# Attention and max-out expert kernel: heads loaded as pairs, split in place and put together by copies and on-chip transfers, with a fixed list of expert products

## Chip, cores and metric

The kernel runs on one core of one Trainium2 chip. The metric is the device time of one execution in microseconds (us); lower is better. Five engines work beside each other: PE multiplies matrices, DVE, ACT and POOL work on vectors (POOL can't read PSUM), and SP here issues nearly all transfers, in program order.

## What is computed

```python
def _attn_ref(q, k, v, s):                     # B, H, S, D = 8, 8, 576, 64
    scores = scale * np.matmul(q, k.transpose(0, 1, 3, 2))
    cum = np.cumsum(np.maximum(s, 0.0), axis=-1)
    bias = -(cum[:, :, :, None] - cum[:, :, None, :])
    scores = np.where(causal, -1e9, scores + np.minimum(bias, 0.0))
    attn = np.exp(scores - np.max(scores, axis=-1, keepdims=True))
    attn = attn / (np.sum(attn, axis=-1, keepdims=True) + 1e-09)
    return np.matmul(attn, v)
...
x = attn_out.transpose(0, 2, 1, 3).reshape(B * S, H * D)        # 4608 x 512
h = np.maximum(np.maximum(x @ w1, x @ w2), x @ w3)              # 4608 x 768
return h @ w_out                                                # 4608 x 512
```

## The kernel before

Attention goes by **visits**: a visit is one batch and one pair of heads (two heads of 64 rows fill 128 partitions). A visit has **steps**, one for each block of 128 queries (qb 0 to 4, the last of 64). Batches 0 and 1 are visited twice, once for qb 0 and 1 and once for qb 2 to 4: 16 visits, 40 steps. Batches 2 to 7 have one visit for each pair with all five blocks: 24 visits (16 to 39), steps 40 to 159. These 24 are called stacked (`stacked`), and the change is about them.

To keep precision with 16-bit products, numbers are split into a high half in fp16 and the low rest. In a stacked visit each head's scores are two products over 128 rows: tile `h` holds the head's (q low, k high) on its own 64 partitions and (q high, k high) on the other 64; tile `l` holds the bias rows on the head's own partitions and (q high, k low) on the others. So each head needs its q and k on both halves of the partitions. Before, the input `qk` has each head twice, one copy under the other. `load_head` (L139) loads 128 x 1152 floats for each head into one of two buffers `raw`; `head_qhi` (L177) and `head_khi` (L181) write the high halves on ACT; `head_qlo` (L186) writes q low on DVE, and POOL copies q high (L190); `head_klo` scales k on POOL (L195) and subtracts (L198); `head_bias` copies the bias rows on POOL. Apart from that, `load_pair` (L289) loads the same pair once more from `pair`, and `pair_max` (L298, DVE) finds its largest magnitudes, from which `pair_scale1` to `pair_scale3` make the batch's scales.

A step t runs: `probs` (reciprocal on DVE, high half of the probabilities on ACT, L716, low half on DVE, L719, then their transposes by SP, L722, and L728 for qb 4), `highest(t+1)` on DVE (L657, L652), the pending evictions, some expert products, `scores(t+2)` on PE (L555, and L566 for qb 4) with `expo(t+1)` on ACT (L676), then the preparations that are due, more expert products, and `values` (L847). Scores have two PSUM buffers, so `scores(t+2)` waits until L719 of step t has read its own.

The experts work on a batch's rows in two sets, of 256 and of 320 columns: 18 groups `pm` (L979, 12 products each), whose maxima DVE takes (L996) and POOL splits (L985, L986), and 4 groups `po` (L1021, 18 products each). How many groups run in a step is in the list `GROUPS` for steps 0 to 59, as (ahead of the scores, behind them). From step 60 on one group goes ahead of the scores and the rest while a running budget (`STEP_NS` for a step, less `pe_cost`) is positive. What is left after step 159 runs at the end.

The order of everything else is the recording order: `at(step, function, ...)` puts a preparation into a step, and the table `moved` shifts single ones by some steps. Each transfer stands in SP's queue where it was recorded, and SP waits at its head.

Of the kernel before, what the change touches and what calls it, by code (L numbers as in the profile page):

```python
# [21 lines left out]
def kernel(  # L22
# [5 lines left out]
    qk: bass.AP,  # L28
# [5 lines left out]
    nc = tc.nc  # L34
# [24 lines left out]
    STEP_NS = 4520.0  # L59
# [80 lines left out]
    def load_head(v, j):  # L140
        b, g, _ = visits[v]
        r = R.setdefault(v, {})
        if v == 2 * NP * NB:
            for n, (x, c0, c1) in enumerate((("rq", 0, S), ("rk", S, 2 * S))):
                r[x, j] = wpool.tile([P, 2 * N], F32, tag=f"w{14 + 2 * j + n}", name=f"{x}{v}_{j}")[:, 0:c1 - c0]
                nc.sync.dma_start(out=r[x, j], in_=qk[b, g, j, :, c0:c1])
            return
        t = io.tile([P, V0], F32, tag="raw", name=f"raw{v}_{j}", bufs=2)
        nc.sync.dma_start(out=t[:, 0:2 * S], in_=qk[b, g, j])
        r["rq", j], r["rk", j] = t[:, 0:S], t[:, S:2 * S]  # L150

    def head_bias(v, j):

        r = R.setdefault(v, {})
        if j == 0:
            h = att.tile([P, 2 * S], F16, tag="qkh", name=f"h{v}_0")
            if v < 2 * NP * NB + 2:
                LOW[v % 2, 0] = att.tile([P, 2 * S], F16, tag="qkl", name=f"l{v}_0")
        else:
            if v < 2 * NP * NB + 2:  # L160
                LOW[v % 2, 1] = wpool.tile([P, 2, 2 * S], F16, tag=f"w{18 + v % 2}", name=f"x{v}_1")
            h = LOW[v % 2, 1][:, 0]
        l = LOW[v % 2, 1][:, 1] if j else LOW[v % 2, 0]
        r["h", j], r["l", j] = h, l
# [8 lines left out]
        nc.gpsimd.tensor_copy(out=l[own, Q4:S], in_=qr[own, g, 4:5].to_broadcast([D, D]))

    def head_qhi(v, j):
        raw, h = R[v]["rq", j], R[v]["h", j]
        nc.scalar.activation(out=h[:, 0:S], in_=raw, func=AF.Copy, scale=QK[visits[v][0]]["q"])  # L177

    def head_khi(v, j):
        raw, h = R[v]["rk", j], R[v]["h", j]  # L180
        nc.scalar.activation(out=h[:, S:2 * S], in_=raw, func=AF.Copy, scale=QK[visits[v][0]]["k"])  # L181

    def head_qlo(v, j):
        raw, h, l = (R[v][x, j] for x in ("rq", "h", "l"))
        far, own = slice((1 - j) * D, (2 - j) * D), slice(j * D, (j + 1) * D)
        nc.vector.scalar_tensor_tensor(  # L186
            out=h[own, 0:S], in0=raw[own], scalar=QK[visits[v][0]]["q"][own], in1=h[own, 0:S],
            op0=ALU.mult, op1=ALU.subtract,
        )
        nc.gpsimd.tensor_copy(out=l[far, 0:S], in_=h[far, 0:S])  # L190

    def head_klo(v, j):
        raw, h, l = (R[v][x, j] for x in ("rk", "h", "l"))
        far = slice((1 - j) * D, (2 - j) * D)
        nc.gpsimd.tensor_scalar(  # L195
            out=raw[far], in0=raw[far], scalar1=QK[visits[v][0]]["k"][far], scalar2=None, op0=ALU.mult
        )
        nc.gpsimd.tensor_tensor(out=l[far, S:2 * S], in0=raw[far], in1=h[far, S:2 * S], op=ALU.subtract)  # L198
# [1235 lines left out]
```

## Time and profile before

| what | value |
|---|---|
| median of 3 runs | 884.27 us (882.59 to 884.44) |
| the profiled execution | 884.48 us, span 882.7 us |
| PE busy | 816.8 us, 93% of the span |
| DVE, ACT, POOL busy | 635.6, 572.7, 403.8 us |
| mean busy share of the DMA engines, queue of SP | 66.3% |
| chain that ended last | PE 22% of the span, DMA 3%, DVE 2%, ACT 1%, POOL 1% |

PE's busy time counts a product from its start to its modelled end, so an idle PE is surely idle, while a busy one may be slow. Idle time of the other engines costs nothing by itself; it matters where it makes PE wait. The span is what lies between the first and last instruction; the execution's time is 1.8 us longer.

### The profile page before, as it was taken

What the parts mean: (1) busy time and instruction counts of PE and PEld (TensorE: products, weight loads), DVE (VectorE), ACT (ScalarE), POOL (GpSimd) and SP (SyncE); (2) the same over time, 40 slices, a digit from 0 to 9 for tenths busy, and PEclk for the clock granted to TensorE, in tenths of its full rate; (3) what the DMA queues carried; (4) which work ended last, traced back from release to release, by engine and by line L of the source; (5) the groups of instructions that cost most, each with busy time, mean ns of one, the idle gap of its engine ahead of it and who ended that gap; (6) DMA issues with size and microseconds to landing.
All of it is one profiled execution on the core that took longest, in us unless ns stands there. A gap on an engine that the chain in (4) does not pass through costs nothing. (4 is left out here: it accounts for less than half of the span.)

```text
span 882.7 us, 19624 instructions
## 1 busy us (share of the span) xinstructions
PE 816.8 (93%) x6929; PEld 617.3 (70%) x6929; DVE 635.6 (72%) x1562; ACT 572.7 (65%) x1506; POOL 403.8 (46%) x580
## 2 busy tenths in 40 slices
PE   5889998899998899998999999999989999999998
PEld 3767777676665578766866677667766678667875
DVE  6979977687878778876868787777868777664110
ACT  5878775677677666766767666667766677765111
POOL 2001115636557446583647555474647555540211
PEclk9999999999999999999999999999999999999999
DMA  9824467998788777878777776777865664645000
GB/s 353 345 88 91 111 136 193 218 179 171 143 202 178 160 163 152 197 150 183 160 180 164 167 146 151 174 151 170 161 156 131 140 137 88 152 78 98 13 13 31
DMA packets 237986, 133.98 MB, mean 152 GB/s; under 512 B 209856, under 2 KB 218560, under 8 KB 237888
## 3 DMA queue, kind: packets, MB, share of 16 engines
q1 hardware_dynamic: 237312, 131.17, 66.3%
q10 hardware_dynamic: 576, 1.57, 0.5%
q8 instruction: 54, 0.88, 0.4%
q14 instruction: 44, 0.36, 0.2%
HBM read 73.43 MB, written 9.44 MB: 94 GB/s over the span
## 5 line engine op out<-in xcount | busy, mean ns | idle before, releaser
L979 PE MATMUL pm<-x,w 128*128 128x320 f16 (+1 forms) x3240 | 426.7, 288 | 6.2 <-DVE x L857 5.1
L979 PEld LDWEIGHTS <-w 128*128 128x128 f16 x3240 | 311.3, 98 | 97.5 <-issue 12.5
L716 ACT ACTIVATE prh<-s,ri 128x512 f16<-128x512 f32 (+3 forms) x272 | 136.4, 548 | 110.8 <-DVE ri L700 95.9
L719 DVE SCALAR_TENSOR_TENSOR prl<-s,ri,prh 128x512 f16<-128x512 f32 (+3 forms) x272 | 147.1, 578 | 50.0 <-ACT prh L716 40.0
L985 POOL CAST hh<-m 128x320 f16<-128x320 f32 (+1 forms) x90 | 48.7, 541 | 230.7 <-DVE m L996 200.6
L676 ACT ACTIVATE s<-s,nm 128x128 f32<-128x128 f32 (+4 forms) x272 | 145.1, 534 | 13.7 <-DVE nm L657 8.8
L996 DVE SCALAR_TENSOR_TENSOR m<-pm,m 128x320 f32<-128x320 f32 (+1 forms) x180 | 82.0, 456 | 93.2 <-PE pm L979 73.4
L1021 PE MATMUL po<-hh,w 128*128 128x320 f16 (+1 forms) x720 | 140.7, 287 | 0.6 <-POOL hh L985 0.5
L1021 PEld LDWEIGHTS <-w 128*128 128x128 f16 x1080 | 104.3, 98 | 35.4 <-issue 6.8
L657 DVE CUSTOM_DVE_ANT_0 s<-s,later,qf 128x128 f32<-128x128 f32 (+1 forms) x192 | 105.9, 552 | 28.0 <-PE s L555 24.3
L1021 PE MATMUL po<-hl,w 128*128 128x320 f16 (+1 forms) x360 | 103.2, 287 | 3.5 <-POOL hl L986 3.3
L195 POOL TENSOR_SCALAR raw<-raw,qf 64x576 f32<-64x576 f32 x46 | 80.5, 1749 | 39.7 <-ACT x L181 37.2
L993 ACT ACTIVATE m<-pm 128x320 f32<-128x320 f32 (+1 forms) x90 | 36.7, 408 | 63.9 <-PE pm L979 62.4
L986 POOL TENSOR_TENSOR hl<-m,hh 128x320 f16<-128x320 f32 (+1 forms) x90 | 70.5, 783 | 7.3
L1029 ACT ACTIVATE o<-po,os 128x320 f32<-128x320 f32 (+1 forms) x60 | 30.0, 500 | 59.4 <-PE po L1021 55.3
L847 PEld LDWEIGHTS <-vh 128*64 128x64 f16 x800 | 44.2, 111 | 22.0 <-issue 15.7
L676 ACT ACTIVATION_READ_ACCUMULATOR s<-s,nm 128x1 f32 x272 | 54.2, 199 | 0.0
L555 PE MATMUL s<-x 128*128 128x128 f16 (+1 forms) x192 | 53.5, 299 | 0.0
L847 PE MATMUL av<-ph,vh 128*64 128x320 f16 (+3 forms) x368 | 48.9, 285 | 1.9 <-DMA ph<-prh 1.7
L847 PE MATMUL av<-ph,vl 128*64 128x320 f16 (+3 forms) x368 | 44.1, 278 | 0.0
L856 ACT ACTIVATE x<-av 128x320 f16<-128x320 f32 (+1 forms) x60 | 24.8, 413 | 22.4 <-PE av L847 21.7
L700 DVE RECIPROCAL ri<-se 128x2 f32<-128x2 f32 (+1 forms) x152 | 23.8, 156 | 21.1 <-ACT se L682 20.3
(225 smaller groups left out, 1276.9 us busy)
## 6 DMA issues: line engine op xcount, KB each, us to landing
raw<-in_qk_dram SPq DMA_DIRECT2D x46, 576.0 KB, 4.4
pair<-in_pair_dram SPq DMA_DIRECT2D x24, 576.0 KB, 4.4
r<-in_w_dram SPq DMA_DIRECT2D x22, 512.0 KB, 7.9
rv<-in_qkv_dram SPq DMA_DIRECT2D x32, 320.0 KB, 3.2
out_dram<-o SPq DMA_DIRECT2D x32, 160.0 KB, 2.0
out_dram<-o SPq DMA_DIRECT2D x32, 128.0 KB, 2.1
raw<-in_qkv_dram SPq DMA_DIRECT2D x8, 480.0 KB, 4.0
ph<-prh SPq DMA_TRANSPOSE x184, 3.6
```

The lines of the kernel that those rows point to most:

```text
L195: nc.gpsimd.tensor_scalar(out=raw[far], in0=raw[far], scalar1=QK[visits[v][0]]["k"][far], scalar2=None, op0=ALU.mult)
L555: nc.tensor.matmul(ps[:, j, :nk], lhsT=w[:, qs], rhs=w[:, S:S + nk], start=(x == "h"), stop=(x == "l"), skip_group_check=True,)
L657: nc.vector.tensor_tensor_reduce(out=sc[:, j], in0=sc[:, j], in1=future[0][:, Q4 - nk:Q4], scale=n, scalar=3.0e38, op0=ALU.add, op1=ALU.mi ...
L676: nc.scalar.activation(out=E[t][:, j, :nk] if plain else sc, in_=sc, func=AF.Exp, bias=nm[:, j:j + 1], scale=-1.0 if below(t) else 1.0, ac ...
L716: nc.scalar.activation(out=hi, in_=src, func=AF.Copy, scale=sc)
L719: nc.vector.scalar_tensor_tensor(out=lo, in0=src, scalar=sc, in1=hi, op0=ALU.mult, op1=ALU.subtract)
L847: nc.tensor.matmul(av[j * D:(j + 1) * D, c0:nq], lhsT=lt, rhs=rt, start=(n < 2), stop=(n >= len(todo) - 2), skip_group_check=True,)
L979: nc.tensor.matmul(pm[:, :nq], lhsT=w[:, wt, kt, :], rhs=xt, start=(n == 0), stop=(n == 3 * NKT - 1))
L985: nc.gpsimd.tensor_copy(out=st["hh"][:, ft, :nq], in_=m1[:, :nq])
L986: nc.gpsimd.tensor_tensor(out=st["hl"][:, ft, :nq], in0=m1[:, :nq], in1=st["hh"][:, ft, :nq], op=ALU.subtract)
L996: nc.vector.scalar_tensor_tensor(out=m1[:, :nq], in0=pm[:, :nq], scalar=HSC, in1=m1[:, :nq], op0=ALU.mult, op1=ALU.max)
L1021: nc.tensor.matmul(pm[:, :nq], lhsT=W[18 + ft][:, wt, dt, :], rhs=st[ht][:, ft, :nq], start=(n == 0), stop=(n == 3 * NFT - 1),)
```

## The change

Inputs: `qk` is gone; `pair` (each pair of heads once, 128 x 1152) is the only source of q and k for stacked visits. One load (`load_nat`) into one of five fixed tiles serves both the maxima and the split. ACT writes q high and k high for both heads at once (`nat_hi`), DVE q low and k low (`nat_lo`), into one staging tile in the order k low, q high, k high, q low. What belongs on a head's own partitions is copied from there by POOL (`nat_own`, four copies of 64 x 576), and what belongs on the other half of the partitions is sent there by SP (`nat_far`, four transfers of 64 x 1152 fp16 from SBUF to SBUF). `h` and `l` hold the same numbers as before, with q and k swapped in `l`, and the score products have the same count and shapes.

```diff
-    def load_head(v, j):
...
-    def head_klo(v, j):
...
+    def fixed(k):
+        if k not in SL:
+            pool, tag = (wpool, f"w{18 + k}") if k < 4 else (io, "raw")
+            SL[k] = pool.tile([P, V0], F32, tag=tag, name=f"fixed{k}", **(dict(bufs=2) if k > 3 else {}))
+        return SL[k]
+
+    def load_nat(v):
         b, g, _ = visits[v]
+        t = fixed((v - 2 * NP * NB) % 5)[:, 0:2 * S]
+        nc.sync.dma_start(out=t, in_=pair[b - NB, g])
+        R.setdefault(v, {}).update(rq=t[:, 0:S], rk=t[:, S:2 * S])
+
+    def staged(v):
+        return fixed(5)[:, 0:2 * S].bitcast(F16).rearrange("p (i c) -> p i c", c=S)
+
+    def nat_hi(v, x):
+        nc.scalar.activation(out=staged(v)[:, 1 + x], in_=R[v][("rq", "rk")[x]], func=AF.Copy, scale=QK[visits[v][0]]["qk"[x]])
+
+    def nat_lo(v, x):
+        u = staged(v)
+        nc.vector.scalar_tensor_tensor(
+            out=u[:, 3 - 3 * x], in0=R[v][("rq", "rk")[x]], scalar=QK[visits[v][0]]["qk"[x]], in1=u[:, 1 + x],
+            op0=ALU.mult, op1=ALU.subtract,
+        )
...
+    def nat_own(v, j, x):
+        own = slice(j * D, (j + 1) * D)
+        nc.gpsimd.tensor_copy(out=R[v]["h"][own, j, x], in_=staged(v)[own, 3 - x])
+
+    def nat_far(v, j, x):
+        own, far = slice(j * D, (j + 1) * D), slice((1 - j) * D, (2 - j) * D)
+        nc.sync.dma_start(out=R[v]["hl"[x]][far, j], in_=staged(v)[own, 1 - x:3 - x])
...
-    PM = (2, 4, 5, 0)
-    VM = 4
+    PM, PM0 = (-25, -21, -17, -13), (20, 22, 24, 26)
+    VM = 2
...
-        at(27 + n, bias4, n)
+        at((27, 28, 41)[n], bias4, n)
...
-        at(o, load_pair, v)
+        o = (PM0[g] if b == NB else first[v - g] + PM[g])
+        at(o, load_nat, v)
         for x in range(2):
-            at(o + (2 if b == NB else PM[x]), pair_max, v, x)
+            at(o + 2 + x, pair_max, v, x)
...
+        for x in range(2):
+            at(first[v] - 6, nat_hi, v, x)
+            at(first[v] - 5, nat_lo, v, x)
+        for j in range(2):
+            at(first[v] - 6, nat_bias, v, j)
+            for x in range(2):
+                at(first[v] - 5, nat_own, v, j, x)
+                at(first[v] - 4, nat_far, v, j, x)
```

`nat_bias` does on POOL what `head_bias` did. The scratch tiles of the bias move to other places in SBUF, and its third part (`bias4`) from step 29 to step 41. `moved` is a new table for the new names. `GROUPS` now has an entry for every step, 0 to 159; entries 0 to 59 differ in a few places, and from step 60 on the budget is no longer used.

What the change moves, at three places. `raw_0` and `raw_1` are the two heads' loads, `fixed` with the destination `h` or `l` is a `nat_far`, `in_pair` a `load_nat`.

SP, around visit 33 (steps 125 to 127), before:

```order
L728 DMA_TRANSPOSE pl_9441<-prl_9595 128x5x64 x2
L149 DMA raw_0_9641<-in_qk_dram 128x1152
L292 DMA pair_9644<-in_pair_dram 128x1152
L722 DMA_TRANSPOSE ph_9683<-prh_9687 128x2x128
L722 DMA_TRANSPOSE pl_9684<-prl_9688 128x2x128
...
L722 DMA_TRANSPOSE ph_9683<-prh_9771 128x4x128
L722 DMA_TRANSPOSE pl_9684<-prl_9772 128x4x128
...
L722 DMA_TRANSPOSE ph_9841<-prh_9845 128x6x128
L722 DMA_TRANSPOSE pl_9842<-prl_9846 128x6x128
...
L149 DMA raw_1_9888<-in_qk_dram 128x1152
```

The same steps in the changed kernel:

```order
L712 DMA_TRANSPOSE pl_9268<-prl_9406 128x5x64 x2
L706 DMA_TRANSPOSE ph_9464<-prh_9468 128x2x128
L706 DMA_TRANSPOSE pl_9465<-prl_9469 128x2x128
L706 DMA_TRANSPOSE ph_9464<-prh_9555 128x4x128
L706 DMA_TRANSPOSE pl_9465<-prl_9556 128x4x128
L129 DMA rv_9611<-in_qkv_dram 128x640
L190 DMA h_9461<-fixed_2650 64x1152
L190 DMA l_2720<-fixed_2650 64x1152
L706 DMA_TRANSPOSE ph_9635<-prh_9639 128x6x128
L706 DMA_TRANSPOSE pl_9636<-prl_9640 128x6x128
L150 DMA fixed_2038<-in_pair_dram 128x1152
```

The loads of single heads are gone from between the transposes. Four short transfers (the two shown, and the same two for the other head) stand behind the transposes of qb 1 and ahead of those of qb 2, and the visit has one load of a pair.

POOL, a part of the preparation of visit 35, before (`m` to `hh` and `hl` are the experts' splits):

```order
L190 COPY l_0_3066<-h_0_9890 64x576
L985 CAST hh_1_9958<-m_1_1_10005 128x320
L986 TENSOR_TENSOR hl_1_9959<-m_1_1_10005,hh_1_9958 128x320
L195 TENSOR_SCALAR raw_0_9641<-raw_0_9641,qf_8555 64x576
L198 TENSOR_TENSOR l_0_3066<-raw_0_9641,h_0_9890 64x576
L170 COPY x_1_3195<-qr_8563 64x512
L173 COPY x_1_3195<-qr_8563 64x64
```

and in the changed kernel:

```order
L998 TENSOR_SCALAR os_0_9682<-p_1_7682,kw 128x1
L179 COPY l_3093<-qr_8550 64x512
L182 COPY l_3093<-qr_8550 64x64
...
L186 COPY h_9764<-fixed_2650 64x576 x4
L969 CAST hh_1_9959<-m_1_0_9871 128x320
L970 TENSOR_TENSOR hl_1_9960<-m_1_0_9871,hh_1_9959 128x320
```

The scaling and the subtraction of k are gone from POOL; a visit has four copies in one row in their place.

PE, where a batch's last values end and its first expert group may begin (steps 97 and 98; first before, then the changed kernel at the same values):

```order
L847 MATMUL av<-pl_8881,vh_8859 64x128
L979 LDWEIGHTS w_721
L979 MATMUL pm_0_0_0_9125<-x_0_7970,w_721 128x256
...
L555 LDWEIGHTS h_0_8715
L555 MATMUL s_9138<-h_0_8715 128x128
```

```order
L831 MATMUL av<-pl_8685,vh_8672 64x128
L1005 LDWEIGHTS w_1194
L1005 MATMUL po_1_1_8961<-hh_1_8415,w_1194 128x320
...
L1005 MATMUL po_1_3_9053<-hh_1_8415,w_1255 128x320
L963 LDWEIGHTS w_721
L963 MATMUL pm_0_0_0_9089<-x_0_7810,w_721 128x256
```

The group that needs these values as its input `x` now comes three groups of the set before later. Over steps 60 to 159 the new list runs one group of 12 products and three of 18 fewer, all of 320 columns; they follow after step 159.

## Rows read from the trace of the kernel before

**Rows 1.** Stretches: us, busy us (count) PE, PEld, DVE, ACT, POOL; clock, DMA share, GB/s

```profile
165.90:322.40 156.50, 144.91 (x1249) 104.29 (x1250) 121.37 (x288) 110.21 (x283) 84.34 (x123) 0.99 0.85 177
322.40:417.10 94.70, 90.83 (x814) 67.66 (x812) 74.72 (x196) 67.84 (x180) 57.01 (x76) 1.00 0.81 169
417.10:513.50 96.40, 91.62 (x826) 68.83 (x824) 74.83 (x197) 67.27 (x180) 55.44 (x74) 1.00 0.76 166
513.50:614.40 100.90, 94.57 (x836) 70.64 (x837) 76.92 (x199) 68.17 (x182) 56.86 (x77) 0.98 0.76 160
614.40:716.30 101.90, 94.79 (x835) 70.54 (x835) 75.18 (x196) 67.83 (x181) 56.09 (x75) 0.98 0.69 147
716.30:806.60 90.30, 87.93 (x782) 65.17 (x783) 64.52 (x171) 61.03 (x163) 42.85 (x53) 1.00 0.53 105
806.60:879.20 72.60, 72.59 (x606) 57.48 (x604) 12.93 (x29) 10.93 (x26) 14.37 (x26) 1.00 0.11 28
```

**Rows 2.** Stretches of 40 us, same columns: two whose granted clock is below 1

```profile
520.00:560.00 40.00, 36.53 (x342) 28.30 (x342) 29.73 (x74) 26.88 (x70) 19.63 (x26) 0.96 0.77 173
640.00:680.00 40.00, 36.52 (x309) 26.23 (x307) 28.48 (x75) 24.86 (x67) 22.88 (x33) 0.96 0.63 147
```

**Rows 3.** Waits of PE, whole span: us in total, times, longest

```profile
PE s L566 <- DVE prl L719: 13.5, 12, 3.3
PE pm L979 <- DVE x L857: 5.1, 5, 1.2
PE po L1021 <- POOL hl L986: 3.3, 5, 1.2
```

**Rows 4.** Waits of SP's queue, whole span: us in total, times, longest

```profile
SPq L149 <- POOL l L198: 20.5, 6, 4.7
```

**Rows 5.** Timeline, POOL and SP, ahead of step 125's transposes: start, us, what

```profile
645.79 1.28 POOL L198 TENSOR_TENSOR l<-raw,h 64x576 f16<-64x576 f32 x1
647.09 0.33 SPq L149 DMA_DIRECT2D raw<-in_qk_dram  x1
```

**Rows 6.** The chain that ended last, steps 125 to 127: start, us, what

```profile
648.84 5.43 DMA ph<-prh
...
655.44 1.15 DVE prl L719 x2
...
656.64 0.68 PE s L566 x8
```

**Rows 7.** Groups by shape: busy us, mean ns, then idle before

```profile
L195 POOL TENSOR_SCALAR raw<-raw,qf 64x576 f32<-64x576 f32 x46 | 80.5, 1749 | 39.7 <-ACT x L181 37.2 <-ACT h L181 0.3
L198 POOL TENSOR_TENSOR l<-raw,h 64x576 f16<-64x576 f32 x23 | 29.9, 1298 | 1.9
L190 POOL COPY x<-x 64x576 f16<-64x576 f16 x24 | 17.8, 742 | 11.4 <-ACT x L177 10.9
L177 ACT ACTIVATE x<-raw,qf 128x576 f16<-128x576 f32 x23 | 17.5, 762 | 0.0
L186 DVE SCALAR_TENSOR_TENSOR x<-raw,qf,x 64x576 f16<-64x576 f32 x23 | 22.2, 966 | 1.9 <-ACT x L177 1.2
L298 DVE TENSOR_REDUCE qm<-pair 128x1 f32<-128x576 f32 x48 | 35.4, 744 | 2.9 <-DMA pair<-in_pair_dram 2.8
```

**Rows 8.** DMA issues: count, KB each, median us from issue to landing

```profile
raw<-in_qk_dram SPq DMA_DIRECT2D x46, 576.0 KB, 4.4
out_dram<-o SPq DMA_DIRECT2D x32, 160.0 KB, 2.0
```

**Rows 9.** Timeline of SP, ends of qb 1's transposes, steps 126 and 146

```profile
654.32 1.21 SPq L722 DMA_TRANSPOSE pl<-prl  x1
...
754.30 1.21 SPq L722 DMA_TRANSPOSE pl<-prl  x1
```

**Rows 10.** The chain, next visit's first scores (steps 130 and 150)

```profile
662.98 0.22 PE s L555 x4
...
760.18 0.22 PE s L555 x4
```

More of the change, by code (lines that the diff above doesn't have):

```diff
@@ L152, in head_bias @@
[L152 to L156, printed above, removed]
-            if v < 2 * NP * NB + 2:
[L158 to L164, printed above, removed]
+    SL = {}
@@ new lines, in nat_hi, with nat_bias @@
+    def nat_hi(v, x):
[6 more added lines that the diff above has]
+        )
+    def nat_bias(v, j):
+        r = R[v]
+        if "h" not in r:
+            h = att.tile([P, 2, 2, S], F16, tag="qkh", name=f"h{v}")
+            if v < 2 * NP * NB + 2:
+                LOW[v % 2] = att.tile([P, 2, 2, S], F16, tag="qkl", name=f"l{v}")
+            r["h"], r["l"] = h, LOW[v % 2]
+        l = r["l"][:, j]
@@ L172, in head_bias @@
         )
[L173 to L190, printed above, removed]
@@ L192, in head_klo @@
-    def head_klo(v, j):
[L193 to L198, printed above, removed]
-    KH, QK, ST, BS, LOW = [], {}, {}, {}, {}
+        nc.gpsimd.tensor_copy(out=l[own, 1, Q4:S], in_=qr[own, g, 4:5].to_broadcast([D, D]))
@@ L203, in load_bias @@
+    def nat_own(v, j, x):
[4 more added lines that the diff above has]
+        nc.sync.dma_start(out=R[v]["hl"[x]][far, j], in_=staged(v)[own, 1 - x:3 - x])
+    KH, QK, BS, LOW = [], {}, {}, {}
     def load_bias():
-        t = wpool.tile([P, V0], F32, tag="w20", name="bias")
-        BS.update(s=t[0:HB, 0:S], c=t[0:HB, S:2 * S], m=t[:, 2 * S:2 * S + 1])
+        t, c = (wpool.tile([P, 2 * N], F32, tag=f"w{14 + i}", name=f"bias{i}") for i in range(2))
+        BS.update(s=t[0:HB, 0:S], c=c[0:HB, 0:S], m=c[:, S:S + 1])
@@ L210, in bias1 @@
         nc.gpsimd.tensor_scalar(out=BS["s"], in0=BS["s"], scalar1=0.0, scalar2=None, op0=ALU.max)
-        t = wpool.tile([P, 2 * V0], F16, tag="w19", name="pieces")[0:HB]
+        t, u = (wpool.tile([P, 4 * N], F16, tag=f"w{16 + i}", name=f"pieces{i}")[0:HB] for i in range(2))
         BS.update(
@@ L283, in bias4 @@
         BS["q", G] = q8
-    def tag_of(v):
-        b, g, _ = visits[v]
-        return (18, 18, 20, 18)[g] if b == NB else 20
-    def load_pair(v):
-        b, g, _ = visits[v]
-        ST[v] = wpool.tile([P, V0], F32, tag=f"w{tag_of(v)}", name=f"pair{v}")[:, 0:2 * S]
-        nc.sync.dma_start(out=ST[v], in_=pair[b - NB, g])
     def pair_max(v, x):
@@ L640, in later_keys @@
     def later_keys():
-        m = wpool.tile([P, Q4 + S], BF16, tag="w23", name="later")
-        nc.gpsimd.memset(m, 0.0)
+        m = wpool.tile([P, 4 * N], BF16, tag="w23", name="later")
+        BS["e"] = m[:, Q4 + S:4 * N]
+        nc.gpsimd.memset(m[:, 0:Q4 + S], 0.0)
         nc.gpsimd.tensor_copy(out=m[:, Q4 - P:Q4], in_=tri)
@@ L1254 @@
             if stacked(v) and f in (load, prep2, prep3):
-                n = v - 2 * NP * NB
-                for j in range(2):
-                    o = first[v] - (8, 5)[j]
-                    if n == 0:
-                        o += 2 - j
-                    elif n == 1 and j == 0:
-                        o += 1
-                    if f is load:
-                        at(o - (3 if n == 0 and j == 0 else 2), load_head, v, j)
-                    elif f is prep2:
-                        at(o, head_bias, v, j)
-                        at(o, head_qhi, v, j)
-                        at(o + 1, head_khi, v, j)
-                    else:
-                        at(o + 1, head_qlo, v, j)
-                        at(o + (1 if n == 0 else 2), head_klo, v, j)
                 continue
@@ L1413 @@
         "start": _np.concatenate([qp[0:nb, :, :, 0:256], pairs(k)[0:nb, :, :, 0:256], wide], axis=3),
-        "qk": _np.concatenate([_np.concatenate([heads(pairs(q), n), heads(pairs(k), n)], axis=4)] * 2, axis=3),
         "pair": _np.concatenate([pairs(q), pairs(k)], axis=3)[nb:],
```

127 lines of the change are left out of this document (63 added, 64 removed), and 16 rows, old and new, of the table GROUPS.

## The prediction, made before the changed kernel was timed

> **What bounds the kernel now.** I read the stretches first, one for each batch of the stacked visits [rows 1]. PE is busy for 90.83 of 94.70 us, 91.62 of 96.40, 94.57 of 100.90 and 94.79 of 101.90, and DVE, the next, for 75 to 77 us. After step 159 PE alone works, 72.59 of 72.60 us. So PE bounds the kernel, and the number of its products is not changed: a change can only take from PE's idle time, or add to it. Idle are 11.6 us in the first stretch, then 3.9, 4.8, 6.3 and 7.1, 33.7 in all, and 2.4 in the last batch, 716 to 807. That last batch is the control in this trace: the loads and splits that the change is about run out in it (POOL busy 42.85 us against 55 to 57, DMA share 0.53 against 0.69 to 0.81), and its idle time is the lowest.
>
> PE pays twice for a long idle stretch. In two 40 us stretches the granted clock is 0.96 [rows 2]: the lacking 0.04 of 40 us is 1.6 us of full clock, or 3.2 us at 1.2 GHz in place of 2.4. A third such stretch stands ahead of them. I count 1.6 us for each.
>
> What PE waits for there is in the waits [rows 3]: 13.5 us for DVE's low half of the probabilities ahead of the scores of qb 4, 5.1 us for an expert input, 3.3 us for POOL's low half of the experts' maxima. The first has a cause far from DVE. SP's queue stood 20.5 us, six times, at a head's load whose buffer POOL had not yet left [rows 4]. One such place in full: POOL subtracts k low from 645.79 to 647.07, the load goes out at 647.09 [rows 5], and only then the transpose behind it, at 648.84, which lands 5.43 us later; ACT waits for that buffer, DVE's halves begin at 655.44, and the scores at 656.64 [rows 6]. The stretch that holds this place is one of the two with the clock at 0.96. This is the wait that the change removes: a load of a pair writes a tile that was last read many steps before.
>
> **The change part by part**, against the profiled execution of 884.48 us (0.21 above the median of 884.27).
>
> 1. Loads. 48 loads of heads go, the 24 of pairs stay; each head load cost SP some 0.33 us [rows 5] and the DMA engines 576 KB [rows 8]. With them goes the standing of rows 4. Of the 13.5 us I take 8.5: the longest waits follow places like that of rows 5 and 6, the short ones are DVE's own queue, which stays. Bounds 0 and 13.5.
>
> 2. Clock. Two of the three dips should go with those waits: 2 x 1.6 = 3.2 us. Bounds 0 and 4.8.
>
> 3. The list. A batch's first group no longer follows the values that it reads; three groups of the set before go ahead of it, as the order rows on PE show. Of 5.1 us I take 4. Bounds 0 and 5.1.
>
> 4. POOL. For each visit it loses two scalings (1749 ns), two subtractions (1298), and two copies of 742, and gains four copies of that kind [rows 7]: 7.58 less 2.97 is 4.6 us, 111 us over 24 visits. POOL is not the bound; what it gives back is rows 3's 3.3 us, of which 2.5 as I take it, since the last group's maximum still comes just ahead. Bounds 0 and 3.3.
>
> 5. ACT does two activations of 762 ns for a visit in place of four [rows 7]: 36.6 us less over 24 visits, hidden under PE, but on the way from scores to the next scores. DVE keeps two subtractions of 966 and two maxima of 744. I take 2 us of PE's remaining waits. Bounds 0 and 7: the 33.7 us of idle time, less the 11.6 of the first stretch, less what items 1, 3 and 4 take, is about 7.
>
> 6. The transfers across. Four for a visit are recorded behind qb 1's transposes, and PE needs them at the next visit's first scores. No row shows a transfer from SBUF to SBUF. For landing, the nearest rows are the store of 160 KB, 2.0 us, and the load of 576 KB, 4.4 us [rows 8]; each transfer moves 64 x 1152 x 2 bytes, 147 KB, so I stay near the store, at 2.5. For SP's time I take 0.4 us each, between 0.33 [rows 5] and a transpose's 1.21 [rows 9], near the first, since both are plain copies. So the last lands 1.6 + 2.5 = 4.1 us after SP is free; with a load's landing it is 6.0. The room: from 654.32 + 1.21 to 662.98 it is 7.45 us, and at a narrow visit, from 755.51 to 760.18, 4.67 [rows 9, 10]. By my value no visit waits, by the other end a narrow one waits 1.3 us; at 24 visits that is 31 us at most. SP also holds qb 2's transposes back by up to 1.6 us, but these come from a later step and are mostly not ready. I take 4 us in all, some 0.65 us (half of 1.3) at a quarter of the visits. Bounds 0 and 31.
>
>    Weighed against a rule, in a sentence that the sum can do without: the Trainium skill, "DMA: Bandwidth & Descriptors", Rules for kernel authors, advises against two transfers to disjoint halves of the partitions, since they serialize, and for one of 128 partitions. That speaks against this part, which sends to both halves; by it the time would be that of the third rival below, 912 us, and no run so far shows it.
>
> 7. Moved without a price: the bias parts and their scratch (`bias4` at step 41) have many steps of lead; the pair's maxima stand earlier or later on DVE with the same count. The cover is DVE's idle fifth [rows 1]; without it, each batch has 8 x 0.74 = 6 us of maxima, but those were there before too.
>
> Sum: 8.5 + 3.2 + 4 + 2.5 + 2 - 4 = 16.2 us less, **868 us**. By the control, if every batch came to the last one's 2.4 us in 90.3, the 5.5 batches from 166 to 716 would keep 14 of 33.7 us: 20 less, and with the clock's 4.8 about 25. My sum is two thirds of that.
>
> **The rivals.**
>
> *All of it.* The waits go as in the last batch and the transfers cost nothing: 884.5 - 25 = 859.5 us. For it: that batch itself. Against it: that batch has less of everything, not only cheaper splits (DVE 64.52 us against 75). Chance 0.12.
>
> *The list starves PE.* Over steps 60 to 159 the list holds 66 products fewer, which follow after step 159. Should DVE, busy for 75 of 95 to 102 us a batch with no less to do, set the pace of the steps as it is, PE idles in them for what it doesn't do there: 72.60 us for 606 products [rows 1] is 0.12 each, 7.9 us in all, and nothing of items 1 to 5 shows: 892 us. It decides where the steps from 60 to 159 don't get 8 us shorter. Against it: in the last batch DVE's steps ran through in 90.3 us. Chance 0.08.
>
> *The transfers go one after another.* If each of the four lands before the next moves, they take 4 x 2.0 = 8.0 us by the store's row to 17.6 by the load's [rows 8], against a room of 4.67 to 7.45, mean 6.1. At 8.0 every visit's first scores wait 2 us: 24 x 2 = 48, less the 20 of items 1 to 5: 912 us. It decides from 20 / 24 = 0.85 us a visit on. Against it: the transpose of rows 6 goes out 1.75 us after the load of rows 5, and such a load takes 4.4 us to land, so that transfers of this queue are in flight together. Chance 0.11. (This mechanism is the rule of the Trainium skill that item 6 names.)
>
> *The waits only change places.* SP's queue is free of loads that stand, but DVE's own queue holds the scores back by as much: 884 us. For it: ACT and POOL are relieved, DVE is not, and PE's waits are put down to DVE. Against it: rows 5 and 6, where DVE waited for ACT, and ACT for SP. Chance 0.11, three quarters of it within 0.2%.
>
> That the change doesn't remove the standing loads is no rival: the order rows show none left between the transposes.
>
> **How the numbers follow.** My forecast has the remaining 0.58, around 868, from 860 to 880 by the bounds of items 1 and 6. The range is 856 to 886: it takes in the case of all and that of changed places, and leaves out the two slow rivals, 0.19. About 0.2%, 1.8 us, is what a measurement here can tell from no change. Faster by more: 0.58 + 0.12 = 0.70. Same: 0.08. Slower: 0.08 + 0.11 + 0.03 = 0.22.
>
> **What would show it.** Item 1: no wait of SP for POOL at a load, and the wait ahead of the scores of qb 4 under 6 us. Item 2: at most one dip of the clock between 240 and 800. Item 3: no wait of `pm` for DVE's `x` half. Item 4: POOL near 290 us busy. Item 6: landings under 3 us, and no wait of the first scores of a visit for a transfer. The steps would end about 24 us earlier and what follows be 8 us longer. I am wrong if PE's idle time from 166 to the end of the steps stays at 30 us or more, or if first scores wait for `h` or `l`.

## The result and the profile after

The changed kernel takes **869.8 us** (median of 4 runs, 867.46 to 874.8); the kernel before, on the same chip, 883.43 (880.95 to 884.44). The ratio (of the means) is 0.9857, with a 95% interval from 0.9808 to 0.9907: 12.6 us less (8.2 to 17.0), against a forecast of 16.2, and 869.8 against 868. The execution profiled took 870.82 us (span 869.0), 13.7 less than the one before.

The stretches of the changed kernel, batch by batch, answer to [rows 1]. Columns: stretch in us, its length, then busy us (count) of PE, PEld, DVE, ACT, POOL, and clock, DMA share, GB/s.

```profile
165.90:321.20 155.30, 142.40 (x1237) 103.09 (x1236) 119.00 (x282) 104.50 (x276) 58.27 (x113) 0.99 0.72 148
321.20:415.50 94.30, 88.64 (x777) 64.88 (x776) 74.90 (x197) 60.53 (x165) 41.45 (x74) 0.98 0.66 144
415.50:510.00 94.50, 93.14 (x836) 69.65 (x837) 76.03 (x200) 63.54 (x177) 35.71 (x66) 1.00 0.69 146
510.00:602.50 92.50, 90.72 (x819) 67.93 (x818) 74.69 (x197) 62.57 (x172) 38.11 (x70) 1.00 0.73 148
602.50:699.80 97.30, 95.72 (x854) 71.61 (x855) 74.84 (x198) 63.44 (x173) 35.71 (x66) 1.00 0.67 137
699.80:785.70 85.90, 85.21 (x779) 64.40 (x777) 62.46 (x170) 57.21 (x157) 27.98 (x46) 1.00 0.48 100
785.70:867.30 81.60, 79.93 (x658) 62.72 (x655) 13.08 (x30) 12.87 (x30) 14.38 (x26) 1.00 0.14 32
```

Read length less PE's busy time. Before, it was 11.6, 3.9, 4.8, 6.3, 7.1 and 2.4 us, 36.1 in all; now it is 12.9, 5.7, 1.4, 1.8, 1.6 and 0.7, 24.0 in all. So idle time gave 12.1 of the profile's 13.7 us: 15.2 after 415 us, less the 3.1 that the first two stretches lost. The seventh row begins behind the last attention steps and is not among these. PE's busy time, summed over the seven rows, is 675.8 us against 677.2. DVE has as much to do as before (74.7 to 76.0 us a batch), ACT some 4 to 7 us less and POOL 15 to 20 us less.

The changed kernel's waits, every engine (us in total, times, longest), against [rows 3] and [rows 4]:

```profile
PE s L538 <- DVE prl L703: 9.9, 18, 1.7
...
PE s L549 <- DVE prl L703: 3.8, 3, 2.8
...
SPq L190 <- POOL h L186: 2.8, 5, 1.4
...
PE pm L963 <- DVE x L841: 0.3, 1, 0.3
...
PEld L538 <- DMA l<-fixed: 0.2, 1, 0.2
```

The scores of qb 4 (L566 before, L549 now) waited 13.5 us for DVE and now wait 3.8. The expert input `x` held `pm` for 5.1 us and now for 0.3. PE's wait for POOL at `po`, 3.3 us before, has no row left. SP's wait for POOL at a load, 20.5 us before, is down to 0.2 at the load of a pair (L150); at a transfer across (L190) it waits for POOL's copies instead, 2.8 us in all. The scores of the other blocks wait more for DVE than they did (9.9 us).

The transfers across and the loads of pairs in the DMA issues (count, KB each, median us to landing), against [rows 8]:

```profile
fixed<-in_pair_dram SPq DMA_DIRECT2D x24, 576.0 KB, 4.6
...
h<-fixed SPq DMA_DIRECT2D x48, 144.0 KB, 3.2
l<-fixed SPq DMA_DIRECT2D x48, 144.0 KB, 3.4
```

SP's queue at one visit (timeline: start, us, what): the four transfers stand between the transposes of qb 1 and qb 2.

```profile
637.44 0.47 SPq L190 DMA_DIRECT2D h<-fixed  x1
637.97 0.59 SPq L190 DMA_DIRECT2D l<-fixed  x1
638.61 0.59 SPq L190 DMA_DIRECT2D h<-fixed  x1
639.24 0.59 SPq L190 DMA_DIRECT2D l<-fixed  x1
639.94 1.30 SPq L706 DMA_TRANSPOSE ph<-prh  x1
```

The new work by shape (busy us, mean ns | idle before), against [rows 7]:

```profile
L186 POOL COPY h<-fixed 64x576 f16<-64x576 f16 x96 | 67.9, 734 | 57.5 <-DVE fixed L161 56.2
L161 DVE SCALAR_TENSOR_TENSOR fixed<-fixed,qf,fixed 128x576 f16<-128x576 f32 x48 | 42.6, 923 | 0.6 <-ACT fixed L157 0.6
L157 ACT ACTIVATE fixed<-fixed,qf 128x576 f16<-128x576 f32 x48 | 35.4, 762 | 0.0
```

The first scores of step 60 and of step 159, in the changed kernel's timeline of PE:

```profile
317.06 0.28 PE L538 MATMUL s<-h 128*128 128x128 f16 x2
...
780.01 0.30 PE L549 MATMUL s<-h 128*64 128x256 f16 x2
```

and in that of the kernel before:

```profile
315.60 0.22 PE L555 MATMUL s<-h 128*128 128x128 f16 x1
...
802.78 0.30 PE L566 MATMUL s<-h 128*64 128x256 f16 x1 [0.31 <-DVE prl L719]
```

From the one to the other it is 463.0 us now and was 487.2. What follows after 780.01, until the last product starts, is 85.3 us and was 76.1: the products that the list moved out of the steps take 9.2 us there. The net is 15 us, and 1.5 are lost again ahead of step 60 (317.06 against 315.60).

### The profile page after: what moved, and what is told of

Its sections match the earlier page's. It is cut to its first block, busy times and chain, and to the rows that moved or that the text cites. A ratio compares the mean times of both kernels' runs of the same rounds, so it can differ in the third digit from the quotient of the medians.

```text
span 869.0 us, 19550 instructions
## 1 busy us (share of the span) xinstructions
PE 815.7 (94%) x6929; PEld 617.2 (71%) x6929; DVE 630.6 (73%) x1562; ACT 541.8 (62%) x1458; POOL 286.4 (33%) x532
## 5 line engine op out<-in xcount | busy, mean ns | idle before, releaser
L703 DVE SCALAR_TENSOR_TENSOR prl<-s,ri,prh 128x512 f16<-128x512 f32 (+3 forms) x272 | 147.0, 577 | 51.7 <-ACT prh L700 30.8
L969 POOL CAST hh<-m 128x320 f16<-128x320 f32 (+1 forms) x90 | 45.7, 508 | 353.0 <-DVE m L980 277.5
L660 ACT ACTIVATE s<-s,nm 128x128 f32<-128x128 f32 (+4 forms) x272 | 144.9, 533 | 17.5 <-DVE nm L641 11.7
L1005 PE MATMUL po<-hh,w 128*128 128x320 f16 (+1 forms) x720 | 142.5, 289 | 0.0
L641 DVE CUSTOM_DVE_ANT_0 s<-s,later,qf 128x128 f32<-128x128 f32 (+1 forms) x192 | 106.0, 552 | 16.8 <-PE s L538 11.3
L186 POOL COPY h<-fixed 64x576 f16<-64x576 f16 x96 | 67.9, 734 | 57.5 <-DVE fixed L161 56.2
L538 PE MATMUL s<-h 128*128 128x128 f16 (+1 forms) x192 | 42.3, 300 | 11.2 <-DVE prl L703 9.9
L161 DVE SCALAR_TENSOR_TENSOR fixed<-fixed,qf,fixed 128x576 f16<-128x576 f32 x48 | 42.6, 923 | 0.6 <-ACT fixed L157 0.6
L538 PE MATMUL s<-l 128*128 128x128 f16 (+1 forms) x192 | 41.9, 299 | 0.0
```

What stands on the lines that cost most here:

```text
L186: nc.gpsimd.tensor_copy(out=R[v]["h"][own, j, x], in_=staged(v)[own, 3 - x])
L538: nc.tensor.matmul(ps[:, j, :nk], lhsT=w[:, c, qs], rhs=w[:, 1 - c, 0:nk], start=(x == "h"), stop=(x == "l"), skip_group_check=True,)
L641: nc.vector.tensor_tensor_reduce(out=sc[:, j], in0=sc[:, j], in1=future[0][:, Q4 - nk:Q4], scale=n, scalar=3.0e38, op0=ALU.add, op1=ALU.mi ...
L660: nc.scalar.activation(out=E[t][:, j, :nk] if plain else sc, in_=sc, func=AF.Exp, bias=nm[:, j:j + 1], scale=-1.0 if below(t) else 1.0, ac ...
L703: nc.vector.scalar_tensor_tensor(out=lo, in0=src, scalar=sc, in1=hi, op0=ALU.mult, op1=ALU.subtract)
L969: nc.gpsimd.tensor_copy(out=st["hh"][:, ft, :nq], in_=m1[:, :nq])
```

## The experiments

Of each the time is given, and the ratio to the kernel before on the same chip. A difference in us is the ratio less one, times the 884.3 us of the kernel before, so that runs of different chips can stand beside each other; by it the change is worth -12.6. Of two kernels that are near each other, the intervals decide. The lengths of steps and the waits are those of the one execution of each kernel that was profiled.

### The standing load alone: `e3_loads_later`

The kernel before, where a table of single moves had put these visits' first head load one step early:

```diff
+    for v in (23, 27, 31, 35, 39):
+        del moved["load_head", v, 0]
```

> The kernel before with five entries of its table of shifts taken out: the first head's load of visits 23, 27, 31, 35 and 39 goes out one step later, behind the next transposes instead of ahead of them, so that SP doesn't stand there for POOL. Theory (SP standing at a load is what holds up the scores of qb 4): SP's wait for POOL's subtraction falls from 20.5 us to under 6, the wait ahead of the scores of qb 4 from 13.5 to under 7, and one or two of the dips of the clock go: 6 to 10 us faster, 874 to 878. Rival (DVE's own queue holds those scores back): both times within 2 us of before. Rival (the later load makes ACT's split late): a wait of ACT for the load, and 2 to 6 us slower.

Measured: 876.11 us, ratio 0.9893 [0.9865, 0.9921], **-9.5 us**. Its waits (SP's queue for the first row):

```profile
SPq L149 <- POOL l L198: 3.2, 3, 2.2
...
PE s L566 <- DVE prl L719: 4.5, 6, 2.8
```

and its two stretches that answer to [rows 2]:

```profile
520.00:560.00 40.00, 38.61 (x374) 30.59 (x372) 31.86 (x81) 29.95 (x79) 22.70 (x30) 1.00 0.78 177
640.00:680.00 40.00, 39.85 (x352) 28.63 (x351) 31.88 (x83) 29.92 (x79) 27.97 (x39) 1.00 0.72 163
```

SP stands 3.2 us for k low where it stood 20.5, and PE waits 4.5 us ahead of qb 4's scores where it waited 13.5. In both stretches the clock, at 0.96 before, is full, and PE is busy for 2.1 and 3.3 us more of the 40. No split was touched, no product, no list: five entries of a table give nearly the size that items 1 and 2 of the forecast have together (11.7). POOL and ACT still do all their old work, so these waits were not the price of that work as such. The execution profiled shows 13.8 us less in steps 60 to 159 (487.2 to 473.4); it lost 5.5 ahead of them (first scores of step 60 at 321.13, against 315.60), where the edit changes nothing.

### The list alone: `e1_list_only`

The kernel before with the changed kernel's 160 entries of `GROUPS` (cut):

```diff
-        (0, 0), (1, 1), (1, 1), (0, 3), (1, 1), (0, 0), (1, 1), (2, 2), (2, 1), (4, 0)]
+        (0, 0), (1, 1), (1, 1), (0, 3), (0, 2), (0, 0), (1, 0), (0, 0), (2, 1), (2, 1), (1, 2), (0, 2), (1,
+        1), (3, 0), (2, 0), (1, 0), (1, 1), (1, 0), (1, 2), (0, 3), (1, 0), (1, 1), (1, 1), (1, 2), (1, 0),
...
```

> The kernel before with the changed kernel's list of expert groups for all 160 steps, and nothing else of the change. Theory (the list and the new splits gain separately): the list alone removes the wait of pm for DVE's x half (5.1 us before, at most 1 here) and leaves SP standing at the heads' loads (20.5 us before, 12 or more here) and the wait ahead of the scores of qb 4; so it gains 3 to 6 us: 878 to 881. Rival (the list needs the new splits; without them it starves PE in the steps, because 66 products fewer stand there): 2 to 8 us slower than before, 885 to 892. Rival (the list is all of the gain): 870.

Measured: 889.73 us, ratio 1.0058 [1.0031, 1.0085], **+5.1 us**. The wait of `pm` for `x` is gone here too, but:

```profile
PE s L555 <- DVE prl L719: 12.3, 11, 1.8
PE s L566 <- DVE prl L719: 11.2, 8, 2.9
```

PE waits 23.5 us ahead of these scores, against 19.3 before (5.8 and 13.5): what it no longer waits at `pm` it waits there. Steps 60 to 159 take 478.3 us (317.50 to 795.77), 8.9 less than before, and what was moved out takes 9.2 behind them: the list by itself wins nothing. The profiled execution, 886.68 us, shows half of the loss only; it was the second fastest of ten.

### The changed kernel without its list: `e2_nat_budget`

```diff
+    GROUPS = GROUPS[:60]
```

so that from step 60 on a budget decides again, with 4580 ns a step where the kernel before has 4520. Entries 0 to 59 stay those of the changed kernel.

> The changed kernel with its list cut to 60 entries, so that from step 60 on the budget (4580 ns a step) fills the steps as it did before. Theory: the splits alone gain what the standing of SP and POOL's late halves cost, 8 to 11 us, and the wait of pm for x comes back (3 to 6 us): 873 to 877. Rival (the list is all of the gain): 881 to 884. Rival (the list gains nothing of its own): 870.

Measured: 877.35 us, ratio 0.9919 [0.99, 0.9937], **-7.2 us**. Its wait for `x` is back:

```profile
PE pm L963 <- DVE x L841: 4.9, 4, 1.2
```

Steps 60 to 159 take 480.6 us here (to 796.43), 17.6 more than with the list. So the list, which costs 5.1 us in the old kernel, brings 5.4 in the new one (-7.2 to -12.6). The two intervals overlap a little; by the medians of the changed kernel and of `e6_first_loads` and `e11_tiles_only` below, which come out as it does and whose intervals lie apart from this one, it is 6.2 to 7.6. And without the list all the rest of the change (-7.2) is no better than the later loads alone (-9.5, overlapping intervals).

### Later loads and the list: `e5_later_and_list`

Both edits above in the kernel before.

> The kernel before with the first head's load of visits 23, 27, 31, 35 and 39 one step later (876.1 us by itself) and with the changed kernel's list for all 160 steps (889.7 by itself, slower than before). No new splits. Theory (the list starved PE only because SP stood at the loads): the two add up to what the changed kernel gains, 868 to 872. Rival (the list needs steps that the lighter ACT and POOL make shorter): no gain over 876, so 876 to 884.

Measured: 881.96 us, ratio 0.9972 [0.9941, 1.0003], **-2.5 us**, 7.0 worse than the later loads alone. Steps 60 to 159 get only 2.2 us shorter by the list (473.4 to 471.2), and the 9 us of products follow behind them: here the rival *The list starves PE* (7.9 us) holds nearly as priced. PE's wait for DVE ahead of the scores of qb 0 to 3 is 11.0 us, 6.6 with the later loads alone. For ACT it waits ahead of the same scores as follows, 9.8 us in all, where it waits 2.0 with the later loads alone and 1.3 in the changed kernel:

```profile
PE s L555 <- ACT s L676: 5.9, 6, 1.2
...
PE s L555 <- ACT se L682: 3.9, 6, 1.5
```

A free queue of SP is not all that the list needs; something else in the change is. The next runs load ACT and POOL, which the change relieves. Two other parts of it were not tried alone: the new table `moved`, and the 48 loads fewer, beside which the transposes of `ph` land in 3.2 us in the changed kernel (median; 3.6 here, 3.5 with the later loads alone).

The three pairs, steps 60 to 159 without and with the list:

| kernel | budget | list | by the list |
|---|---|---|---|
| before | 487.2 | 478.3 | -8.9 |
| before, later loads | 473.4 | 471.2 | -2.2 |
| changed kernel | 480.6 | 463.0 | -17.6 |

In each the list adds 9 to 10 us behind step 159.

### ACT's and POOL's relief: `e8_act_load`, `e9_pool_small`, `e7_pool_load`, and a control

To the changed kernel, work on scratch tiles is added where a visit's splits stood: on ACT five activations of 128 x 112 for each visit, on POOL scalings and subtractions of 64 x 112 (ten of each in `e7_pool_load`, six in `e9_pool_small`).

```diff
+    def extra_pool(v, j):
+        far = slice((1 - j) * D, (2 - j) * D)
+        for _ in range(3):
+            nc.gpsimd.tensor_scalar(
+                out=EX["a"][far], in0=EX["a"][far], scalar1=QK[visits[v][0]]["k"][far], scalar2=None, op0=ALU.mult
+            )
+            nc.gpsimd.tensor_tensor(out=EX["b"][far], in0=EX["a"][far], in1=EX["b"][far], op=ALU.subtract)
...
+            at(first[v] - (6, 4)[j], extra_pool, v, j)
```

> The changed kernel with ACT's saved time put back: for each stacked visit five activations of 128 x 112 on the same scratch, two at 6 and three at 4 steps ahead of the visit, some 1.5 us of ACT in place of the two activations of 128 x 576 that went. Theory (ACT's relief is worth some 2 us of PE's waits): 1 to 4 us slower than the changed kernel, 871 to 874. Rival (ACT is on the way from scores to scores in every step, and its relief is most of what makes the list work): 876 or more. Rival (nothing): within 1 us.

Measured: 879.43 us, ratio 0.9955 [0.9926, 0.9983], **-4.0 us** where the changed kernel has -12.6. ACT's busy time went up from 541.8 to 579.1 us, by 37.3, a fifth more than the change takes from it (572.7 to 541.8, by 30.9). Its waits:

```profile
PE s L557 <- DVE prl L722: 14.4, 26, 2.0
...
PE s L568 <- DVE prl L722: 6.4, 6, 3.0
```

They were 9.9 and 3.8 us. The rows name DVE, which has nothing more to do; it waits for ACT's high half of the probabilities, 50.6 us in all against 30.8. Steps 60 to 159 last 468.4 us, 5.5 more than in the changed kernel. So a load on ACT somewhat larger than the relief costs some 9 us beside this list, where item 5 took 2.

> The changed kernel with POOL's old work put back as work on a scratch tile that nothing waits for: for each stacked visit ten scalings and ten subtractions of 64 x 112 in two rows, at the steps 6 and 4 ahead of the visit, as many columns as the two scalings and two subtractions of 64 x 576 before. Theory (POOL's relief counts only through the experts' low halves, 3.3 us of waits before): po waits for hl again, 2 to 4 us, and 2 to 5 us slower than the changed kernel, 872 to 875. Rival (POOL's relief counts for nothing): within 2 us of 870. Rival (it is most of the gain, through DVE, which is slower beside a busy POOL): 877 or more, with DVE's subtractions over 900 ns in place of 812.

Measured: 924.73 us, ratio 1.0456 [1.0401, 1.051]. The load was mis-sized: 145.9 and 99.7 us of it, since a scaling of 64 x 112 took 608 ns and a subtraction 415. It tells that POOL's queue can stop the steps (PE waited 21.8 us for POOL at `po`), and nothing of what POOL's relief was worth. One reading holds: DVE's subtractions beside that load took 881 ns, not more than the 923 of the changed kernel (both means; the 812 of the expectation is a median).

> The changed kernel with six small scalings and six small subtractions of a scratch tile more on POOL for each stacked visit, put where the heads' splits stood: 24 x 6 x (608 + 415 ns, as the run with ten of each measured them) = 147 us, about what the change took away from POOL in the first 40 to 160 steps. It says what POOL's relief is worth by itself. If POOL's relief is worth little (forecast item 4, 2.5 us, that is the experts' low halves coming late): 871 to 875 us, PE's wait for the low halves of the maxima back near 3 us. If nothing: 868 to 872. If POOL's relief carries a large part of the gain, as the run with the heavier load would have it: above 880 us, with PE's waits for DVE's low half of the probabilities above 10 us.

Measured: 887.57 us, ratio 1.0033 [1.0012, 1.0054], **+2.9 us**: the whole gain is gone. POOL's busy time rose by 141.7 us (286.4 to 428.1), a fifth more than the 117.4 that the change takes from it (403.8 to 286.4). PE's waits:

```profile
PE s L557 <- DVE prl L722: 12.4, 16, 2.5
...
PE po L1024 <- POOL hh L988: 4.2, 5, 1.3
PE s L568 <- DVE prl L722: 3.5, 2, 2.8
PE s L580 <- DVE prl L722: 2.9, 2, 1.6
...
PE po L1024 <- POOL hl L989: 2.5, 5, 0.6
```

`po` waits 6.7 us for the halves of the maxima; these waits have no row in the changed kernel. Steps 60 to 159 last 475.2 us (316.25 to 791.41), 12.2 more than the changed kernel's 463.0. (The profiled execution, 882.33 us, was the fastest of twelve.) Neither the 2.5 us of item 4 nor "nothing" stands; the expectation of more than 880 us does, though PE's waits for DVE grew less (4.6 us, by the three such rows) than those for POOL.

The control has the scratch tiles, cleared once, and no added work.

> The two kernels with a load added to ACT or to POOL, without the load: the scratch tiles stand in SBUF and are cleared once, nothing else. A control for both. If those two lost their 10 and 18 us by the work itself, this one stands where the changed kernel does: 868 to 872 us. If the tiles' place in SBUF, or simply any change of the program, costs as much as the load did: 877 us or more.

Measured: 871.15 us, ratio 0.986 [0.9828, 0.9891], **-12.4 us**: what the two loads lost, they lost by their work. Neither brings back the waits for ACT that `e5_later_and_list` has (0.7 us with ACT's load, 1.3 with POOL's): that a relief of ACT and POOL is what makes the list pay is likely by these runs, not shown.

### More relief for ACT: `e10_k_hi_pool` and `e12_k_hi_pool_early`

POOL scales k (128 x 576) in place of ACT; in the second kernel one step earlier for three of a batch's four visits, and two for the six of them whose entry in `moved` is deleted.

```diff
     def nat_hi(v, x):
+        if x:
+            nc.gpsimd.tensor_scalar(
+                out=staged(v)[:, 2], in0=R[v]["rk"], scalar1=QK[visits[v][0]]["k"], scalar2=None, op0=ALU.mult
+            )
+            return
...
+    for v in (21, 22, 26, 30, 34, 38):
+        del moved["nat_hi", v, 1]
...
-            at(first[v] - 6, nat_hi, v, x)
+            at(first[v] - 6 - (x if g else 0), nat_hi, v, x)
```

> The changed kernel with k's high half (both heads at once, 128 x 576) made by POOL in place of ACT, in the same step: 24 activations of 762 ns leave ACT (18 us of its 542) and 24 scalings of about 1.75 us join POOL (42 us to its 286). In the run with a loaded ACT 37 us more there cost about 10 us. If ACT's work is still in the way of the steps, half of that comes back per us: 2 to 5 us faster than the changed kernel, 865 to 868 us. If ACT was no longer in the way: 868 to 872. If POOL makes k high too late for DVE's low half and the transfers across, first scores of a visit wait for them, and it is slower: above 874 us.

Measured: 878.44 us, ratio 0.9935 [0.9912, 0.9957], **-5.7 us**, so 7 us worse than the changed kernel, with ACT's busy time down by 14.0 us. The scaling takes 1871 ns, 44.9 us for 24, and DVE's subtractions stand for it, 7.5 us in all:

```profile
L166 DVE SCALAR_TENSOR_TENSOR fixed<-fixed,qf,fixed 128x576 f16<-128x576 f32 x48 | 45.7, 981 | 7.5 <-POOL fixed L158 7.5
```

> The changed kernel with k's high half made by POOL in place of ACT, as in the run before, but one step earlier for three of a batch's four visits (the first has its scale only then), so that DVE's subtraction no longer stands for it (7.5 us, six times, in that run). If the 8.6 us that run lost came from k's high half coming late to DVE: 866 to 871 us, no wait of DVE for POOL's scaling above 2 us in all, and ACT's 14 us less may bring 1 to 3 us below the changed kernel. If they came from POOL's 42 us of added work standing ahead of what the experts need: 875 to 880 us as before.

Measured: 872.25 us, ratio 0.9872 [0.9841, 0.9903], **-11.3 us**: the interval holds the changed kernel's 0.9857. DVE has no wait for this scaling any more:

```profile
L166 DVE SCALAR_TENSOR_TENSOR fixed<-fixed,qf,fixed 128x576 f16<-128x576 f32 x48 | 43.4, 945 | 0.0
```

The same scalings (42.3 us of POOL here), with 14 us less of ACT, come out even with the changed kernel. Between the two runs only their place in the queues differs, so it is the place, not POOL's sum, that cost `e10_k_hi_pool` most of its 7 us. No version here beats the changed kernel.

### The transfers one step later: `e4_far_later`

```diff
-                at(first[v] - 4, nat_far, v, j, x)
+                at(first[v] - 3, nat_far, v, j, x)
```

> The changed kernel with the four transfers across recorded one step later, behind the transposes of qb 2. In the changed kernel the median room from the end of qb 1's transposes to the next visit's first scores is 8.7 us, the four take 2.6 us of SP and the last lands 3.4 us after its issue, 6.0 in all, so some 2.7 us are left; one step later about 5.7 us of room are gone. Theory (the transfers overlap and land 6 us after SP is free, with little to spare): the first scores of each of 24 visits wait 2 to 3.5 us for h or l: 48 to 84 us slower than the changed kernel, 918 to 954. Rival (they land long before they are needed): within 3 us of 870. Rival (they go one after another, 4 x 3.4 us): 24 x 10, over 1000.

Measured: 898.54 us, ratio 1.0165 [1.0135, 1.0194], **+14.6 us**, 28.7 more than the changed kernel's median. First scores now wait, by these rows of PE:

```profile
PE s L538 <- DMA h<-fixed: 12.7, 11, 2.3
...
PE s L538 <- DMA l<-fixed: 5.0, 14, 0.6
```

28.7 us over 24 visits are 1.2 us a visit, less than the 2 to 3.5 expected, and they are not spread evenly: in the execution profiled, 15.9 us are lost ahead of step 60 (whose first scores start at 332.94, against 317.06), 12.2 in steps 60 to 159. A transfer lands in 2.7 to 2.8 us (median). A step's delay costs about the upper bound of item 6, 31 us.

### The first loads of pairs: `e6_first_loads`

```diff
-    PM, PM0 = (-25, -21, -17, -13), (20, 22, 24, 26)
+    PM, PM0 = (-25, -21, -17, -13), (20, 23, 24, 26)
```

> The changed kernel with the second of the first batch's loads of pairs in step 23 in place of 22, so that it no longer goes out right behind a load of v and the load of s. In the changed kernel's trace SP's transpose at 142.5 us then took 3.7 us to issue, ACT waited 1.5 us for its landing, and PE idled 2.3 us at 148.8. Theory (the three loads together fill the queue): that idle time is under 1 us and the time 1 to 3 us under the changed kernel's, 867 to 869. Rival (the load only moves its crowd one step on): no difference beyond the spread of runs, 869 to 871.

Measured: 870.58 us, ratio 0.9845 [0.9803, 0.9887], **-13.7 us**: no difference from the changed kernel. PE's idle time at that place did fall, from 2.3 to 0.4 us, and the time did not follow.

## Why the prediction was right, and which terms were not

The time, the place of the gain and the shift of the end came as forecast: steps end 22.8 us earlier (some 24 were named), idle time falls to 24.0 us (wrong from 30 on), and the time from the last scores to the last product grows by about 9 (8). The total was 3.6 us too large, and some terms were off by more than that, in both directions. Set beside the runs, items 1 and 2 (11.7) gave 9.5 us, and items 3 to 6 (4.5) gave 3.1. Within these sums the terms don't hold: to the 3.1 the list came with 7.0 lost and the rest with 10.1 won, where 4 and 0.5 were added. That they came out so near is partly luck.

**Item 1, the standing loads (8.5), and item 2, the clock (3.2).** The chain of [rows 5, 6] was read rightly: undone alone, it gives 9.5 us, and with it both stretches of [rows 2] come back to full clock. The changed kernel, too, has full clock there (the last two of these rows), and qb 4's scores wait 3.8 us where under 6 was forecast. But item 2's count was missed, since the changed kernel has two stretches of half clock between 240 and 800, not one. The first two of these rows of its stretches of 40 us show them, one in each:

```profile
280.00:320.00 40.00, 35.77 (x305) 25.34 (x300) 30.21 (x81) 26.80 (x72) 12.85 (x26) 0.96 0.69 150
...
320.00:360.00 40.00, 37.45 (x346) 29.99 (x344) 31.87 (x86) 25.11 (x72) 17.85 (x30) 0.96 0.61 135
...
520.00:560.00 40.00, 38.98 (x368) 31.18 (x366) 32.34 (x84) 28.56 (x78) 14.01 (x26) 1.00 0.74 155
...
640.00:680.00 40.00, 39.57 (x359) 29.07 (x354) 31.53 (x82) 26.26 (x73) 15.99 (x32) 1.00 0.71 137
```

In the first, PE is idle for 4.2 of 40 us, in the second for 2.6. Two dips went and one came: 1.6 us, half of the term. That count differs between executions: the profiles of `e6_first_loads` and `e11_tiles_only`, whose times are the changed kernel's, have one stretch below full clock there, 280 to 320. And over the whole execution the clock gave nothing. These are the spans and mean granted clocks of the kernel before, the changed kernel and `e3_loads_later`:

```profile
core 0: 882.7 us, clock 0.990
...
core 0: 869.0 us, clock 0.988
...
core 0: 874.5 us, clock 0.984
```

So the clock does come back where a long wait goes, but in these two executions more of it is missing elsewhere, most of it ahead of 240 us (0.91 from 80 to 120 us in the changed kernel, 0.96 before). The term of 3.2 us does not show in the total.

**Item 3, the list (4).** The wait that it was priced by went, 5.1 to 0.3 us. Yet its worth is no property of the list: 5.1 us lost in the old kernel, 5.4 won in the new one. The step that failed is the sum itself, which added items 3, 4 and 5 as if each could be had alone. The list takes 9 us of products out of the steps, and that is a gain only if the steps then run more than 9 us shorter; in the table above they do so only in the changed kernel.

**Item 4 (2.5) and item 5 (2).** POOL's busy time of 286.4 us was forecast (near 290), and four copies for a visit at 734 ns (742). The price was not. Item 4's 2.5 us were read from the wait of `po` for POOL; that wait is gone with the list alone, beside all of POOL's old work (no such row in `e1_list_only` and `e5_later_and_list`, 2.5 us in `e3_loads_later`), so it was no measure of what POOL's relief gives. With a load put back beside the new list, ACT's costs 8.6 us (-12.6 to -4.0) and POOL's 15.5 (-12.6 to +2.9); item 5's upper bound, 7 us of idle time left over in the old order, is below the first. Each load is a fifth larger than the relief, is made of many small instructions, and stands at the old splits' steps but not in their place among the neighbours; `e12_k_hi_pool_early` shows that place matters. So 8.6 and 15.5 are the prices of these loads at that place, not of the relief in general. From the later loads with the list to the changed kernel it is 10.1 us (-2.5 to -12.6), where items 4, 5 and 6 had 0.5. That step holds the relief of ACT and POOL, but the fewer loads, the transfers and the new `moved` too; what each gives stays open.

**Item 6, the transfers (-4).** A transfer takes 3.2 to 3.4 us to land, not 2.5 (under 3 was forecast), and 0.59 us of SP, not 0.4; both lie between the ends that the rows of before set. (The upper bound of 31 us took SP's time at its low end; at the other, 1.21, the narrow room would have been short by 4.6 us, and 24 visits by 110.) Four of them, with 0.64 us from one to the next, and the landing of the last make 3 x 0.64 + 3.4 = 5.3 us, more than the 4.67 of the narrow room of [rows 9, 10]. Yet PE waits 0.2 us for them in all. What failed is the room: a quarter of the visits was taken to be narrow, by one visit. Before, over the visits from step 65 on, the room is 7.7 us in the mean, and the visit with the 4.67 of [rows 9, 10] has the least of all. In the changed kernel it is 9.0, at least 7.6 (6.1 with the earlier visits); without the list 8.0, at least 6.5. At the visit that was narrow, step 150, the last transpose of qb 1 now ends at 728.29 + 1.22, and the next visit's first scores start 8.7 us later, in these rows of the timelines of SP and PE:

```profile
728.29 1.22 SPq L706 DMA_TRANSPOSE pl<-prl  x1
...
738.25 0.28 PE L538 MATMUL s<-h 128*128 128x128 f16 x2
```

So the term, 4 us, was nothing, and the mis-sized part of it was not the transfer. That each of these transfers lands before the next moves is refuted. Four issues within some 1.9 us land after 3.2 and 3.4 us (medians over 48 each, `h` and `l`), by their order in the four after 3.1, 3.3, 3.3 and 3.5; one behind the other, those issued later would show a multiple of the first one's time. The rival with 912 us falls. With it falls, as that rival reads it, the rule of the Trainium skill that the prediction weighs ("DMA: Bandwidth & Descriptors", Rules for kernel authors: two transfers to disjoint halves of the partitions serialize). How much the four slow each other down is not shown, since no run sends one transfer of 128 partitions in their place.

**The first stretches.** They gain nothing: 12.9 and 5.7 us idle against 11.6 and 3.9. The forecast took nothing from the first, but expected the second to move toward the last batch's level, and it went the other way. Moving the second of the first loads a step (`e6_first_loads`) does not change the time; why the second stretch is worse stays open.

**The rivals.** *All of it* (859.5) named the right limit: from 415 us on the idle time is below the last batch's old 2.4 us; but the early stretches kept theirs. *The waits only change places* is partly seen: the scores of qb 0 to 3 wait 9.9 us where they waited 5.8. *The list starves PE* is wrong for the changed kernel, and nearly right for the old one with its loads later (7.0 us for 7.9).

## What to carry to other kernels

Look for the instruction that stands at the head of an in-order queue before pricing a rewrite: here five entries of a table, which let a load be issued one step later, give 9.5 us where the whole change gives 12.6 (the intervals overlap). Don't add up the prices of edits that share a step: a list that takes work out of the steps costs 5 us in the old kernel and brings 5 in the new one, so try it together with the other edits. An engine that is busy for little over a third of the time (POOL, 38% in `e10_k_hi_pool`) can still cost several us, by where its work stands in its queue; ask which work of the critical engine stands behind it, not how full it is.

## What was not expected of the hardware

The SBUF to SBUF transfers of 144 KB overlap and land in 3.2 to 3.4 us (2.7 to 2.8 in `e4_far_later`), 0.59 us of SP each. On POOL small instructions are dear: a scaling of 64 x 112 takes 608 ns (`e7_pool_load`), and one of 64 x 576, with five times the columns, 1749 [rows 7]. And where PE's long wait was removed, the clock came back with it, at the two places that `e3_loads_later` shows; the mean clock of that whole execution is lower all the same, 0.984 against 0.990.
